# A convolution by Fourier stages beside a gated linear unit: three stages on sums and differences about the middle, and split tokens kept in DRAM

## The chip, the cores and the metric

The kernel runs on one core of a Trainium2 chip. A core has five engines that run their own lists of instructions in order: PE multiplies matrices (its weight loads are the profile's PEld), DVE and ACT work element by element, POOL and SP here mostly issue DMA transfers. The metric is the time of one execution on the device in microseconds (us), the median of several runs.

## The reference

For 2048 tokens of 512 channels the reference computes a gate per token and mixes two branches with it. Branch a is a long convolution of each channel with a kernel built from 128 complex exponentials; branch b is a gated linear unit with 1792 hidden columns.

```python
g = _sigmoid((x * gate_w).sum(-1, keepdims=True))
P = jnp.exp((A * dt[:, None])[:, :, None] * pos[None, None, :])
K = 2.0 * jnp.einsum("dn,dnl->dl", C, P).real
Kf = jnp.fft.rfft(K, 2 * L); Uf = jnp.fft.rfft(u_t, 2 * L)
a = jnp.fft.irfft(Uf * Kf[None, :, :], 2 * L)[:, :, :L] + u * D_skip
b = jnp.einsum("bsf,fd->bsd", (x @ w_gate) * (x @ w_up), w_down)
return g * a + (1 - g) * b
```

## The kernel before, in words

**The gated unit (GLU).** The 1792 hidden columns are 14 tiles f of 128, in five groups (3, 2, 3, 3, 3). Per group, the tokens come as four chunks of 512, so there are 56 steps (one f, one chunk). All three matrices are split into a rounded high part and a low part, and every product is three matmuls (high-low, low-high, high-high). In `hidden` a step has 24 matmuls into the PSUM tiles `pg` and `pu`; their product h is split again by ACT and DVE (`hh`, `hl`), and `down` multiplies it with the split down weights into `y`, 36 matmuls for a chunk and a group of three. A step's results go to DRAM through `acc`; from the second group on by an accumulating DMA of POOL. `tokens` loads 256 KB of one token tile (`raw<-in_xT`), ACT rounds it (`xhi`), DVE subtracts (`xlo`): 16 such tiles in the first group and 12 in each of the other four, since a group begins with the chunk that the one before ended with. Five buffers hold the split token tiles, and a chunk needs four.

**The convolution.** Its 4096-point transform is cut in stages of matmuls between transposes through DRAM. `u_part` reads the tokens and multiplies them with `w1` (8 batches of 4 matmuls, 512 columns each); the result goes to the DRAM tensor `su_d`. For each of 16 blocks of 32 channels DVE and ACT build tables of powers `x` and `v`; `k_block` multiplies them on PE (64 matmuls, "k<-v,x"), and ACT copies the result to `kt` with a transposed order. After every fourth block a quarter q of the channels is ready: `k_first` (two batches with `w1k`) fills `sk_d`; `transforms(q)` runs four batches `m_second` with `w2` on `su_d` and `sk_d`, the complex products `m_product` on DVE, two batches `m_inverse` with `w3` whose results are stored in `y_d`, and `m_last`, which reads `y_d` back (in four loads of 512 KB) and multiplies with `w4`. ACT scales by the gate, and POOL adds the result to the output. All these batches work in the four PSUM banks named `k`, and PE's array is used as several small tiles: for example 64 rows by 32 columns, eight at a time, in `m_second` (`tile_position`).

**Order.** Nothing is left to chance: every piece of work is entered in a list with its engine, a duration, what it reads and writes, and a rank. `Work.run` walks through these with the given durations and writes down the instructions of each engine in the order in which it lets them start. GLU products have the lowest rank and a due time (`T_STEP` times the number of the step, less 5 us). On the chip, each engine then keeps that order and waits by semaphores. The weights of the skip connection (`D_skip`) are loaded once into `skip`, as 4 blocks of 4 short runs. SP issues nearly all loads and stores, one after the other in its own order. A transfer's landing is told by one of eight semaphores, taken in turn, and SP waits for the transfer eight before it on the same semaphore.

Of the kernel before, what the change touches and what calls it, by code (L numbers as in the profile page):

```python
# [10 lines left out]
F32 = mybir.dt.float32  # L11
# [7 lines left out]
P = 128  # L19
# [23 lines left out]
N2 = list(range(1, 32, 2)) + list(range(2, 32, 4)) + list(range(0, 32, 8)) + list(range(4, 32, 8))  # L43
K_COLS = [[(0, 16, 16)], [(32, 8, 40), (48, 4, 52), (56, 4, 60)]]

def fourier_matrices():

    n1, k1 = np.arange(64), np.arange(64)
    ang = 2 * np.pi * np.outer(n1, k1) / 128
    c = np.stack([np.cos(ang), -np.sin(ang)], 2)
    c[:, 0, 1] = (-1.0) ** n1
    c = c.reshape(64, P)
    w1 = np.tile(c, (2, 1))
    w1k = np.tile(np.stack([c[2 * np.array(K_ROWS) + b] for b in range(2)], 1), (4, 1, 1))
    n2, k2 = np.array(N2), np.arange(32)
    w2 = np.zeros((2, 2, 32, 32, 2, 32))  # L60
    w3 = np.zeros((4, 32, 8, 2, 2, 2, 32))
    w4 = np.zeros((P, 64))
    s = 1 / 4096
    for k in range(64):
        S, j, e = k // 8, k // 2 % 4, k % 2
        q = k // 2
        if k:
            ph = 2 * np.pi * np.outer(n2, k + 128 * k2) / 4096
            co, si = np.cos(ph), np.sin(ph)
            w2[e, 0, :, q, 0], w2[e, 1, :, q, 0] = co, si  # L70
            w2[e, 0, :, q, 1], w2[e, 1, :, q, 1] = -si, co
            w3[j, :, S, e, 0, 0], w3[j, :, S, e, 0, 1] = 2 * s * co.T, 2 * s * si.T
            w3[j, :, S, e, 1, 0], w3[j, :, S, e, 1, 1] = -2 * s * si.T, 2 * s * co.T
            w4[2 * k], w4[2 * k + 1] = np.cos(ang[:, k]), -np.sin(ang[:, k])
            continue

        for l in range(1, 32):
            h, f = (0, 128 * l) if l < 16 else (1, 64 + 128 * (l - 16))
            ph = 2 * np.pi * n2 * f / 4096
            co, si = np.cos(ph), np.sin(ph)  # L80
            w2[0, h, :, 0, 0, l], w2[0, h, :, 0, 1, l] = co, -si
            w3[0, l, 0, 0, 0, h], w3[0, l, 0, 0, 1, h] = 2 * s * co, -2 * s * si
        w2[0, 0, :, 0, 0, 0], w2[0, 0, :, 0, 1, 0] = 1.0, (-1.0) ** n2
        w3[0, 0, 0, 0, 0, 0], w3[0, 0, 0, 0, 1, 0] = s, s * (-1.0) ** n2
        w4[0], w4[1] = 1.0, (-1.0) ** n1

    w4 = w4.reshape(2, 4, 2, 2, 4, 64).transpose(0, 2, 1, 3, 4, 5).reshape(P, 64)
    parts = (w1, w1k, w2.reshape(P, 32, 64), w3.reshape(P, 8, 2, 2, 64), w4)
    return [np.ascontiguousarray(a, np.float32) for a in parts]
# [24 lines left out]
T_STEP = 10.3  # L114
# [169 lines left out]
def gated_mix_kernel(  # L284
# [32 lines left out]
    m_su, m_sk, m_y, m_out = (work.memory() for _ in range(4))  # L317
# [12 lines left out]
    def inp(shape):  # L330
        return new("mid", "in", shape, bufs=3)
# [4 lines left out]
    half_pi = const.tile([P, 1], F32, name="half_pi")  # L336
    shift = const.tile([P, 1], F32, name="shift")
    gate = const.tile([P, NR], F32, name="gate")
    ngate = const.tile([P, NR], F32, name="ngate")
    score = const.tile([P, NR], F32, name="score")  # L340
# [4 lines left out]
    w1_t = tpool.tile([P, P], F32, name="w1_t")  # L345
    w1k_t = tpool.tile([P, 2, P], F32, name="w1k_t")
    skip = tpool.tile([P, 4, 32], F32, name="skip")
    m_const, m_powers, m_w1, m_w1k, m_skip = (work.memory() for _ in range(5))
# [3 lines left out]
    gw = new("mid", "bd", [P, D])  # L352
# [22 lines left out]
    def split(hi, lo, s, key):  # L375
# [5 lines left out]
        ph, pl = (hi, s), (lo, s)  # L381
        at = lambda x: x.t if s is None else x.t[:, s * D : (s + 1) * D]
        add("act", 0.62, lambda: act.copy(at(hi), src()), r=[got], w=[ph], rank=0)
        add(
            "dve", 0.69,
            lambda: dve.tensor_tensor(out=at(lo), in0=src(), in1=at(hi).bitcast(F32), op=ALU.subtract),
# [14 lines left out]
    def first_loads():  # L401
        in_y = lambda shape: new("mid", "y", shape, bufs=2)
        in_ev = lambda shape: new("mid", "ev", shape, bufs=3)
# [10 lines left out]
        for f in (1, 2):  # L414
            load_two(lambda k, f=f: ("w", f, k), in_ev, wts[f][:, : 2 * D].rearrange("p (k d) -> p k d", k=2))
# [51 lines left out]
    def product(pg, which, w, x, kt, after, first):  # L467
# [5 lines left out]
        def fn():  # L473
            for n, (a, b) in enumerate(three):
                pe.matmul(
                    pg.t, w[a].t[:, base : base + P], x[b].t, start=kt == 0 and n == 0, stop=kt == KT - 1 and n == 2
                )

        add("pe", 0.681, fn, r=[(w[0], part), (w[1], part), x[0], x[1]], w=[pg], rank=2, after=after)
# [62 lines left out]
    def ends():  # L542
# [7 lines left out]
        for r, y in ending:  # L550
# [4 lines left out]
                    out=sums.t[:, r, P * (KT - 1) :], in0=sums.t[:, r, P * (KT - 1) :], in1=late["fin"].t[:, r],  # L555
# [49 lines left out]

    def u_part(c):
        ut = inp([P, 2, D])
        add("sp", 0.42, lambda: sp.dma_start(ut.t, uv[:, 2 * c : 2 * c + 2, :]), w=[ut], dma=512, after=9.0 + 15.0 * c)

        def score_of(j):  # L610
            r = 2 * c + j
# [4 lines left out]
                    pr.t, ut.t[:, j, :], 1.0, gw.t, op0=ALU.mult, op1=ALU.mult, accum_out=score[:, r : r + 1]  # L616
                ),
                r=[ut, gw], w=[pr, (m_gate, ("s", c // 2))], rank=0,
            )


# [701 lines left out]
```

## Time and profile before

| | |
|---|---|
| median of 3 runs | 618.17 us (617.34 to 620.17) |
| span of the profiled execution | 615.6 us |
| PE busy | 605.5 us (98%) |
| DVE busy | 514.9 us (84%) |
| ACT busy | 420.1 us (68%) |
| DMA | 121.67 MB, 198 GB/s |

The profiled execution has no time of its own beside its span, from the first instruction to the last; the median of the runs is 2.6 us longer. Busy time is the time in which at least one instruction of an engine runs; "idle before" is what the engine waited ahead of a group. All work goes through one recording helper, so the rows carry its line, L100 (L120 after the change), and are told apart by the names of the tiles: out<-in. Names are shown without buffer numbers, so that `w_t` stands for `w1_t` and `w4_t`. An fp32 matmul shows as two records; a GLU matmul (fp32r) as one. A row of the chain of waits gives its start, its length, and the engine and tile that the time went to.

### The profile page before, as it was taken

The numbers are of one execution on the slowest core, as the hardware profiler recorded it, in microseconds if no ns is written. First come the engines' busy times: TensorE is split into PE (matmuls) and PEld (weight loads), VectorE is DVE, ScalarE is ACT, GpSimd is POOL, SyncE is SP. The second block draws the span as 40 slices with busy tenths as digits, with TensorE's granted clock in tenths as the row PEclk, the third lists the DMA queues.
The fourth block names the chain that finished last, engine by engine and source line by source line (L and its number), as shares of the span: only waits on it lengthen the run. The fifth ranks groups of instructions, "written<-read, shape, count | busy, mean of one in ns | idle before, by whom it ended". The sixth has DMA issues, their size and how long they took to land.

```text
span 615.6 us, 17970 instructions
## 1 busy us (share of the span) xinstructions
PE 605.5 (98%) x7524; PEld 468.9 (76%) x7524; DVE 514.9 (84%) x810; ACT 420.1 (68%) x953; POOL 88.6 (14%) x125
## 2 busy tenths in 40 slices
PE   8999999999999999999999999999999999999996
PEld 5776777788777788887768888786888887678865
DVE  6958999999999999999889999999999842377342
ACT  5469877896878886679688768878885663533320
POOL 0211111111112201010120202021110101210120
PEclk9999999999999999999999999999999999999999
DMA  8795736555677977748797939787996789897771
GB/s 284 221 283 181 242 111 199 171 180 119 158 198 189 234 206 191 172 121 206 245 229 181 235 112 229 221 239 167 196 237 194 188 232 308 205 278 199 170 107 69
DMA packets 103238, 121.67 MB, mean 198 GB/s; under 512 B 6644, under 2 KB 66548, under 8 KB 102900
## 3 DMA queue, kind: packets, MB, share of 16 engines
q1 hardware_dynamic: 83732, 92.33, 49.3%
q0 software_dynamic: 19008, 28.06, 25.4%
q8 instruction: 59, 0.97, 0.6%
q14 instruction: 23, 0.19, 0.1%
q10 hardware_dynamic: 416, 0.13, 0.1%
HBM read 69.37 MB, written 51.12 MB: 196 GB/s over the span
## 4 chain that ended last, share of the span: by engine, by line
PE 75%; issue 10%; DMA 7%; DVE 4%; ACT 3%; POOL 1%; POOLq 0%; ACTq 0%; DVEq 0%
PE pg L100 20%; PE y L100 19%; PE pu L100 19%; PE k L100 18%; DMA out<-acc 3%; DMA raw<-in_xT 3%; ACT acc L100 1%; ACT ts L100 1%; DMA y<-in_xT 1%; DVE xlo L100 1%; POOL out L100 1%; ACT rt L100 1%; POOL su_d L100 1%; DVE v L100 1%; DVE t L100 1%
## 5 line engine op out<-in xcount | busy, mean ns | idle before, releaser
L100 POOL DMA_DIRECT2D out<-acc x60 | 51.3, 891 | 369.1 <-ACT acc L100 327.2
L100 PE MATMUL y<-dhi,hl 128*128 128x512 f32 x224 | 90.7, 405 | 1.5 <-ACT acc L100 0.9
L100 PE MATMUL pg<-xhi,wlo 128*128 128x512 f32 x224 | 90.3, 403 | 0.4 <-ACT h L100 0.3
L100 PE MATMUL pg<-xlo,whi 128*128 128x512 f32 x224 | 87.8, 392 | 1.6 <-issue 1.2
L100 PE MATMUL pu<-xhi,wlo 128*128 128x512 f32 x224 | 89.3, 399 | 0.0
L100 PE MATMUL pg<-xhi,whi 128*128 128x512 f32 x224 | 87.7, 392 | 0.5 <-ACT whi L100 0.5
L100 PE MATMUL y<-dhi,hh 128*128 128x512 f32 x224 | 87.5, 390 | 0.0
L100 PE MATMUL y<-dlo,hh 128*128 128x512 f32 x224 | 87.4, 390 | 0.0
L100 PE MATMUL pu<-xhi,whi 128*128 128x512 f32 x224 | 87.4, 390 | 0.0
L100 PE MATMUL pu<-xlo,whi 128*128 128x512 f32 x224 | 87.4, 390 | 0.0
L100 ACT ACTIVATE acc<-y,ngate 128x512 f32<-128x512 f32 x76 | 51.8, 692 | 29.9 <-PE y L100 18.4
L100 DVE TENSOR_TENSOR h<-pu,h 128x512 f32<-128x512 f32 x56 | 38.5, 688 | 39.7 <-PE pu L100 39.4
L100 ACT CAST hh<-h 128x512 fp32r<-128x512 f32 x56 | 34.9, 623 | 38.3 <-DVE h L100 38.2
L100 ACT COPY ts<-k 128x512 f32<-128x512 f32 (+1 forms) x112 | 47.7, 503 | 13.8 <-PE k L100 13.7
L100 PEld LDWEIGHTS y<-dhi,hl 128*128 128x128 f32 x224 | 42.0, 188 | 18.6 <-issue 2.7
L100 PEld LDWEIGHTS pg<-xhi,wlo 128*128 128x128 f32 x224 | 42.1, 188 | 18.1 <-issue 7.8
L100 ACT COPY h<-pg 128x512 f32<-128x512 f32 x56 | 32.9, 588 | 30.7 <-PE pg L100 24.5
L100 PEld LDWEIGHTS pu<-xhi,wlo 128*128 128x128 f32 x224 | 42.0, 188 | 12.7 <-issue 3.0
L100 PEld LDWEIGHTS pg<-xhi,whi 128*128 128x128 f32 x224 | 42.1, 188 | 12.5 <-ACT whi L100 2.1
L100 PEld LDWEIGHTS y<-dhi,hh 128*128 128x128 f32 x224 | 42.0, 188 | 9.3
L100 PEld LDWEIGHTS pu<-xhi,whi 128*128 128x128 f32 x224 | 42.2, 188 | 9.0
L100 PEld LDWEIGHTS pg<-xlo,whi 128*128 128x128 f32 x224 | 42.2, 188 | 8.8 <-DVE xlo L100 0.7
(109 smaller groups left out, 1169.5 us busy)
## 6 DMA issues: line engine op xcount, KB each, us to landing
raw<-in_xT SPq DMA_DIRECT2D x60, 256.0 KB, 4.6
out<-acc POOLq DMA_DIRECT2D x60, 256.0 KB, 6.7
raw<-in_wts SPq DMA_DIRECT2D x36, 256.0 KB, 4.4
su_d<-ts POOLq DMA_DIRECT2D x32, 256.0 KB, 4.6
y_d<-ts SPq DMA_DIRECT2D x16, 512.0 KB, 4.7
sk_d<-ts SPq DMA_DIRECT2D x14, 512.0 KB, 5.3
in<-sk_d SPq DMA_DIRECT2D x12, 512.0 KB, 6.8
in<-su_d SPq DMA_DIRECT2D x12, 512.0 KB, 5.4
```

The costliest lines, as they stand in the source:

```text
L100: got = getattr(self.engine, name)(*args, **kw)
```

## The change

**Sums and differences.** A transform of a sequence about its middle falls into a part of the sums of mirrored points and one of their differences, each with half the matrix.

- `u_part` now takes four token tiles at a time (four loads of 1 MB). DVE forms sums and differences of mirrored tiles (two instructions of 1024 elements and four of 512 per load); two batches of 8 matmuls follow, each 32 rows by 64 columns, 8 tiles of the array at a time. POOL stores the result in 32 transfers as before; these now write runs of 2 KB.
- `k_block`: ACT copies half of the result, DVE writes sum and difference (two instructions of 256 elements per block), with a step of 32 elements between neighbours in `kt`. The table `v` has another order, so that ACT and DVE write some of its parts with steps of 2 and 4 elements.
- `m_second`: 32 matmuls of 256 columns on 16 tiles of 32 by 32, in place of 64 of 128 columns on 8 tiles. `su_d` and `sk_d` are read side by side into one tile.
- `m_last`: 16 matmuls of 512 columns on 8 tiles of 64 by 32, in place of 8 on two tiles of 128 by 64. ACT copies the odd half, DVE forms sum and difference, and the gate is applied in place.
- `k_first`, `m_inverse` and the table products of `k_block` keep their columns.

**Layouts in DRAM.** The lines of `sk_d` and `su_d` are permuted: a store now goes out as 4 blocks of 32 lines. `m_last` reads `y_d` in two loads of 1 MB (for the first three quarters), each as 2 blocks of 64 lines: even lines into the lower 64 partitions, odd lines into the upper.

**Tokens.** High and low part of a token tile share one tile `xs`. In the first group of f it is stored to DRAM after the split (16 stores of 512 KB); from the second group on, 48 loads of 512 KB replace load and split.

**Room and pace.** `in` has 2 buffers instead of 3, `ev` 2, and some small tiles share space; `T_STEP` is 9.85 instead of 10.3.

What stands in SP's row at the end of the first quarter, ahead of `m_last`. Before (`in<-y_d` and `y<-y_d` are the four loads of `m_last`):

```order
L100 DMA raw_3590<-in_xT 128x512
L100 DMA w3s_3597<-in_w3 128x512
L100 DMA w3s_3602<-in_w3 128x512
L100 DMA raw_3609<-in_xT 128x512
L100 DMA y_d_59<-ts_3592 128x8x128
L100 DMA pb_3651<-par_d_90 128x128 x2
L100 DMA y_d_59<-ts_3626 128x8x128
L100 DMA in_3818<-y_d_59 128x2x512
L100 DMA in_3820<-y_d_59 128x2x512
L100 DMA in_3822<-y_d_59 128x2x512
```

The same place of the changed kernel:

```order
L120 DMA y_d_59<-ts_3424 128x8x128
L120 DMA y_d_59<-ts_3443 128x8x128
L120 DMA pb_3584<-par_d_88 128x128 x2
L120 DMA in_3600<-y_d_59 128x1x2048
L120 DMA in_3612<-y_d_59 128x1x2048
L120 DMA xs_3677<-xs_d_60 128x1024
L120 DMA xs_3684<-xs_d_60 128x1024
L120 DMA xs_3701<-xs_d_60 128x1024
L120 DMA xs_3713<-xs_d_60 128x1024
L120 DMA sk_d_58<-ts_3715 4x32x1024
L120 DMA sk_d_58<-ts_3736 4x32x1024
```

Two loads of 1 MB stand where four of 512 KB stood, and behind them now come the loads of the next chunk's split tokens (`xs`) and then the stores of the next quarter's `sk_d`, written as 4 blocks.

On PE, the first product that reads the first of these token tiles, in the changed kernel (`xs_3285` was loaded ahead of the two loads of `y_d`):

```order
L120 MATMUL pg_3740<-xs_3285,wlo_1633 128x512
L120 MATMUL pg_3740<-xs_3285,whi_1623 128x512 x2
L120 MATMUL y_3709<-dhi_2618,hl_3734 128x512
L120 MATMUL y_3709<-dlo_2635,hh_3728 128x512
L120 MATMUL y_3709<-dhi_2618,hh_3728 128x512
L120 MATMUL y_3724<-dhi_2618,hl_3734 128x512
L120 MATMUL y_3724<-dlo_2635,hh_3728 128x512
L120 MATMUL y_3724<-dhi_2618,hh_3728 128x512
L120 MATMUL pg_3740<-xs_3677,wlo_1633 128x512
L120 MATMUL pg_3740<-xs_3677,whi_1623 128x512 x2
L120 MATMUL pg_3740<-xs_3684,wlo_1633 128x512
L120 MATMUL pg_3740<-xs_3684,whi_1623 128x512 x2
```

From the end of the second inverse batch of this quarter to the first product with `xs_3677` there are 102 GLU matmuls and two Fourier batches on PE (before, the split of `raw` by ACT and DVE stood between load and product). `m_last` of quarter 0 on PE, with the rows around it; before:

```order
L100 MATMUL y<-dhi,hl 128x512
L100 MATMUL y<-dlo,hh 128x512
L100 MATMUL y<-dhi,hh 128x512
L100 MATMUL k<-in,w_t 64x512 x6
L100 MATMUL k<-y,w_t 64x512 x2
L100 MATMUL pg<-xhi,wlo 128x512
```

and after:

```order
L120 MATMUL pg<-xs,whi 128x512 x2
L120 MATMUL pu<-xs,wlo 128x512
L120 MATMUL pu<-xs,whi 128x512 x2
L120 MATMUL k<-in,w_t 32x512 x16
L120 MATMUL pu<-xs,wlo 128x512
L120 MATMUL pu<-xs,whi 128x512 x2
```

The eight matmuls became sixteen with 32 instead of 64 rows of output, and the batch now stands inside the products of a step. In the changed kernel it stands 156, 159 and 84 GLU matmuls and four, four and three batches behind the second inverse batch of quarters 0, 1 and 2. In quarters 1 and 2, 18 GLU matmuls after `m_last` begins the next new token tile is read that was loaded behind it in SP's row.

The diff, cut to what is spoken of:

```diff
-T_STEP = 10.3
+T_STEP = 9.85
+U_STEP = 20.0
...
     def inp(shape):
-        return new("mid", "in", shape, bufs=3)
+        return new("mid", "in", shape, bufs=2)
...
     def tokens(gi, ci, kt):
-        x = xs[kt] = [new("glu", n, [P, D], F32R, 5) for n in ("xhi", "xlo")]
+        x = xs[kt] = new("glu", "xs", [P, 2, D], F32R, 5)
+        if gi:
+            add("sp", 0.42, lambda: sp.dma_start(x.t.bitcast(F32), xs_d[ci, kt]), r=[(m_xs, (ci, kt))], w=[x], dma=512, rank=0)
+            return
         load(("x", gi, ci, kt), xT[kt * P : (kt + 1) * P, ci * D : (ci + 1) * D])
-        split(x[0], x[1], None, ("x", gi, ci, kt))
+        split(x, x, (0, 1), ("x", gi, ci, kt))
+        add("sp", 0.42, lambda: sp.dma_start(xs_d[ci, kt], x.t.bitcast(F32)), r=[x], w=[(m_xs, (ci, kt))], dma=512, rank=2)
...
+            add("pe", 1.08, fn, r=[(ut, 2 * s), (ut, 2 * s + 1), w1_t], w=banks, rank=1, hold=[st])
...
-                    lambda h=h, n2=n2, st=st: pool_q.dma_start(
-                        su_d[:, :, n2, :].rearrange("f p d -> p f d"), st.t[:, h].rearrange("p (f d) -> p f d", f=KT)
+                    lambda q=q: pool_q.dma_start(
+                        su_d[q, :, n0 : n0 + 4, :].rearrange("(t a) n d -> a t (n d)", a=4),
+                        st.t[:, q].rearrange("p n d -> p (n d)"),
...
-        add(
-            "act", 1.09,
-            lambda: act.copy(
-                kt.t[:, :, g0 : g0 + 8].rearrange("p n g -> p g n"), pk.t.rearrange("p (g j) -> p g j", j=64)
...
+        add("act", 0.6, lambda: act.copy(side(1), pv(0)[:, :, :, ::-1]), r=[pk], w=[(kt, (1, b % 4))])
+        for h, op in enumerate((ALU.add, ALU.subtract)):
+            add(
+                "dve", 0.45, lambda h=h, op=op: dve.tensor_tensor(out=side(h), in0=pv(1), in1=side(1), op=op),
...
-                        sk_d[q, :, n0 : n0 + 8, :],
-                        st.t.rearrange("p n c g -> p n (c g)"),
+                        sk_d[q, :, n0 : n0 + 8, :].rearrange("(t a) n d -> a t (n d)", a=4),
+                        st.t.rearrange("p n c g -> p (n c g)"),
...
-        add("pe", 2.13, fn, r=[*ins, w], w=banks[0] + banks[1], rank=1, hold=tos, many=apart_of(q))
+        add("pe", 1.15, fn, r=[*parts, w], w=banks, rank=1, hold=[to], many=apart_of(q))
...
-            t = inp([P, 1, 2, 4, P]) if r < 12 else new("mid", "y", [P, 1, 2, 4, P], bufs=2)
-            rows_y = y_d[q].rearrange("k (h r) d -> k h r d", h=2)[:, :, r : r + 4]
+                t = inp([P, 16, P])
+                add(
+                    "sp", 0.42,
+                    lambda t=t, g=g: sp.dma_start(
+                        t.t, y_d[q].rearrange("(k p) n d -> p k (n d)", p=2)[:, :, 16 * P * g : 16 * P * g + 16 * P]
+                    ),
+                    r=[(m_y, (q, T)) for T in range(4)], w=[t], dma=1024,
+                )
```

More of the change, by code (lines that the diff above doesn't have):

```diff
@@ L40, with place, first @@
 K_ROWS = [0, 8, 16, 24] + [i for i in range(32) if i % 8]
-N2 = list(range(1, 32, 2)) + list(range(2, 32, 4)) + list(range(0, 32, 8)) + list(range(4, 32, 8))
-K_COLS = [[(0, 16, 16)], [(32, 8, 40), (48, 4, 52), (56, 4, 60)]]
+def place(tq, t, s1, s2):
+    n1 = 63 * s1 + (1 - 2 * s1) * np.arange(32)
+    pair = 2 * (4 * t + tq)
+    return n1, 31 - pair if s2 else pair
 def fourier_matrices():
[L52 to L60, printed above, removed]
+    k1, th = np.arange(64), 2 * np.pi / 4096
+    def first(a, halves):
+        re, im = np.cos(2 * np.pi * np.outer(a, k1) / 128), -np.sin(2 * np.pi * np.outer(a, k1) / 128)
+        im[:, 0] = np.sin(np.pi * a)
+        order = np.arange(64).reshape(32, 2).T.reshape(64)
+        re, im = re[:, order], im[:, order]
+        return np.concatenate([re, im, -re], axis=1)
+    w1 = np.tile(first(np.arange(32) - 31.5, 2), (4, 1))
+    rows = np.array(K_ROWS)
+    w1k = np.tile(np.stack([first(2 * rows + b - 31.5, 1) for b in range(2)], 1), (4, 1, 1))
+    t = 2 * np.arange(16) - 15.5
+    w2 = np.zeros((2, 2, 2, 16, 32, 32))
@@ L316, in gated_mix_kernel @@
     y_d = dram.tile([KT, P, 32, P], F32, name="y_d")
-    m_su, m_sk, m_y, m_out = (work.memory() for _ in range(4))
+    xs_d = dram.tile([4, KT, P, 2, D], F32, name="xs_d")
+    m_su, m_sk, m_y, m_out, m_xs = (work.memory() for _ in range(5))
     pools = {n: open_pool(n, b, PSUM) for n, b in (("ps_y", 2), ("ps_g", 1), ("ps_k", 4))}
```

470 lines of the change are left out of this document (262 added, 208 removed).

## The prediction

> **What bounds the kernel now.** I read the page's busy times first, then windows of 25 us, then the chain of waits, then the groups by engine and shape, then the transfers. Page and windows (in a window: busy us of PE, PEld, DVE, ACT, POOL, then clock, DMA share, GB/s):
>
> ```profile
> PE 605.5 (98%) x7524; PEld 468.9 (76%) x7524; DVE 514.9 (84%) x810; ACT 420.1 (68%) x953; POOL 88.6 (14%) x125
> 100.00:125.00 25.00, 25.00 (x228) 18.35 (x227) 24.42 (x44) 20.50 (x54) 3.14 (x5) 1.00 0.50 157
> 425.00:450.00 25.00, 25.00 (x466) 20.46 (x465) 23.91 (x37) 22.89 (x66) 6.08 (x6) 1.00 1.00 185
> ```
>
> PE is never free at full clock, and DVE has 0.6 to 1.1 us left of 25. So PE work that is removed counts one to one, as long as DVE and the transfers deliver. The chain gives the prices on PE (start, length, what, records):
>
> ```profile
> 61.45 1.92 PE k L100 x8
> 309.89 3.58 PE k L100 x16
> 356.06 2.00 PE k L100 x124
> 359.64 2.72 PE pg L100 x12
> 398.62 1.93 PE k L100 x16
> ```
>
> Twelve GLU matmuls take 2.72 us, 0.227 each. A batch `u_part` (8 records of 4 matmuls) takes 1.92, `m_last` (16 records of 8) 3.58, `k_first` 1.93, `m_second`, `m_inverse` and the table products 2.00. The first and the last three have 1024 columns on each small tile, `m_last` 2048: about 1.9 us per 1024 columns, whatever the tile's shape.
>
> **PE.** `u_part` goes from 1024 to 512 columns per tile: 8 x 0.96 = 7.7 us less. `m_second` from 1024 to 512: 16 x 1.00 = 16.0. `m_last` from 2048 to 1024: 4 x 1.79 = 7.2. The rest keeps its columns. Sum 30.9. No row has 16 tiles at work; the nearest are those with 8 (`m_second` by 64x32, `m_inverse` by 32x64), which go by their columns, so I take the halved price. The other end is that a 32x32 batch still takes 2.00: 16 us less gain. A gain beyond the columns I exclude, since no shape shows one.
>
> **DVE, ACT and the other transfers.**
>
> ```profile
> L100 DVE TENSOR_TENSOR xlo<-raw,xhi 128x512 fp32r<-128x512 f32 x60 | 40.2, 686 | 10.1 <-ACT xhi L100 9.9
> L100 DVE TENSOR_TENSOR y<-ev 128x1024 f32<-128x1024 f32 x16 | 19.5, 1221 | 3.8 <-ACT ev L100 3.3
> L100 DVE COPY ts<-k 128x256 f32<-128x256 f32 x4 | 1.4, 418 | 3.4 <-PE k L100 3.4
> L100 ACT CAST xhi<-raw 128x512 fp32r<-128x512 f32 x60 | 36.6, 622 | 12.7 <-DMA raw<-in_xT 11.8 <-PE pu L100 0.2
> L100 ACT COPY kt<-k 128x512 f32<-128x512 f32 x16 | 18.0, 1127 | 15.4 <-PE k L100 15.3
> L100 ACT COPY ts<-k 128x512 f32<-128x512 f32 x60 | 31.8, 595 | 8.2 <-PE k L100 8.2
> L100 DVE MEMSET v<- 128x32 f32 x2 | 0.1, 85 | 0.1
> L100 DVE MEMSET half_pi<- 128x1 f32 x1 | 0.1, 59 | 0.0
> ```
>
> DVE loses 48 splits of 0.686 = 32.9 us. It gains in `u_part` 8 x 1.22 + 16 x 0.69 = 20.8, in `k_block` 32 x 0.42 = 13.4, in `m_last` 14 x 0.69 + 4 x 0.42 = 11.3. Net +12.6 on 514.9: 527.5 us, 90% of 585, against 84. It fits, with little to spare: while tables are built it already runs at 96 to 98%, so 0 to 13 us may come through. I take nothing, since PE will wait elsewhere (below). ACT loses 48 x 0.62 and, in `kt`, 16 x some 0.5 us, and gains about 5: some 32 us less, which nobody waits for.
>
> The writes of `k_block` and of `v` with steps could cost more. ACT's transposed `kt` does: 1127 against 595 ns for the same 512 elements, 1.04 ns more for each. Were it so on DVE, 32 x 256 plus 16 x 1536 elements would add 34 us. DVE's own nearest row says no: the memset of 32 elements that lie 64 apart takes 85 ns against 59 for one, 0.84 ns each. I take none. [...]
>
> The tokens add 48 x 256 KB of loads and 16 x 512 KB of stores, 21 MB to 121.7. At the mean share (75% busy) that is hardly free, but the runs are 4 KB long and the loads have a chunk's time; I cost them at nothing, up to 10 us where a load is late. The stores of `su_d` become 4 blocks of 2 KB runs; quarter 0 reads them some 100 us later, so a slower landing costs nothing.
>
> **What is late next: loads in two blocks.** This is the term that decides.
>
> ```profile
> skip<-in_dsk SPq DMA_DIRECT2D x1, 2.0 KB
> ...
> GB/s 0 146 0 0 0 0 0 0 2341 0 0 0 1317 0 0 0 0 0 0 0 0 0 146 0 0 0 0 0 0 0 0 0 0 146 0 2341 0 0 0 0
> DMA packets 7, 0.01 MB, mean 161 GB/s; under 512 B 4, under 2 KB 5, under 8 KB 7
> ...
> q1 hardware_dynamic: 489, 1.69, 74.1%
> ...
> y_d<-ts SPq DMA_DIRECT2D x16, 512.0 KB, 4.7
> in<-y_d SPq DMA_DIRECT2D x9, 512.0 KB, 6.5
> out<-kt SPq DMA_DIRECT2D x4, 256.0 KB, 2.0
> ```
>
> All transfers of before but one have an outermost count of 128, 256 or 32, which 16 engines can share evenly. The one is `skip`: 4 blocks of 4 runs of 128 B. The second and third rows are a window of 0.035 us in its transfer (135.597 to 135.632 us): its four packets under 512 B come one after the other, 9 to 10 ns apart, as on one engine, where 16 engines would have had one packet each. The nearest row for a transfer of 2 blocks is thus one that uses as many engines as it has blocks. From 548.3 to 554.2 us, where the 1 MB of `kt<-out` move in runs of 8 KB, queue q1 moved 1.69 MB at 74.1% of 16 engines: 1.69 / (0.741 x 16 x 5.9) = 24.2 KB per us and engine. So 1 MB on two engines takes 21.7 us, where the four loads of 512 KB landed after 6.5; the pair, on the same two, 43.4; and a store of `sk_d` (4 blocks) 5.4 us on four. The other end: spread over 16 engines, the pair takes 5.4 us and nothing below happens.
>
> [...]
>
> Each engine works off SP's queue in order, so what SP issues behind the pair and spreads over all 16 also waits for the two: the `xs` loads. SP itself stops at the eighth transfer behind the first of the pair, which waits on the same semaphore. From the end of the second inverse batch: eviction 4 x 0.595 = 2.4, store 4.7, pair 43.4, landing 2.0 (the quickest row) = 52.5 us. Against this PE has, in the changed order:
>
> - Quarter 0: 102 GLU matmuls and two batches, 23.1 + 3.9 = 27.0 us, before the first `xs` issued behind the pair is read. Wait 25.5, and 1.4 for the load itself: 26.9.
> - Quarter 1: 159 and four batches before `m_last`, 36.0 + 7.9 = 43.9: wait 8.6. Then 18 GLU matmuls and the batch (6.0) until an `xs` that queues behind three stores of `sk_d` (16.2) and takes 1.4: 11.6. The next `xs` queues behind a fourth store: about 6. Together 26.
> - Quarter 2: 84 and three batches, 19.0 + 5.9 = 24.9: wait 27.6. Then two stores (10.8 + 1.4 - 6.0): 6.2. Together 34.
>
> Quarter 3 reads `y_d` in blocks of 32 lines and is spared. DVE and ACT wait with PE, since the tables have few buffers, so nothing is worked ahead. Sum 87 us.
>
> **Sum.** 615.6 - 30.9 + 87 = 671.7 us of span. The median of the runs stands 2.6 us over the profiled span: 674.
>
> **Rivals.**
>
> - *The loads spread as before* (faster). Then 615.6 - 30.9 + 2.6 = 587, and with DVE's lag and some late `xs` up to 603; say 592. For it speaks that PE's cut is sure; against it, `skip`'s packets. It decides at the pair's time: below 12 us all waits vanish. Chance 0.17.
> - *Only `m_last` waits*, the `xs` loads pass the pair. Then quarter 0 has 156 matmuls and four batches, 43.3 us: 52.5 - 43.3 = 9.2, plus 8.6 and 27.6: 45 us, and 632. No row shows a transfer that overtakes. Chance 0.16.
> - *DVE pays for steps* and the loads are quick: 587 + 34 = 621, no gain left. Chance 0.05, half of it within the bound.
> - The forecast: 0.62.
>
> **Numbers.** Half a percent is about what a measurement of this kernel tells from none. Slower: 0.62 + 0.16 + 0.02 = 0.80; within: 0.03; faster 0.17. For the range of the likeliest case the price per engine counts: by the whole run's row of q1,
>
> ```profile
> q1 hardware_dynamic: 83732, 92.33, 49.3%
> q0 software_dynamic: 19008, 28.06, 25.4%
> ```
>
> it is 92.33 MB / (0.493 x 16 x 615.6 us) = 19.0 KB per us: the pair takes 55 and a store 6.9, 11.8 x 3 + 1.5 x 5 = 43 us more, 717; q0's quarter of the engines on top makes 740. Down it goes to 640 with shorter queues. The second rival, and part of the first rival's upper end, take it to 610.
>
> **What would show it.** In the profile after: `in<-y_d` landing after 20 to 45 us and not 7 (right), or under 8 (then the forecast is wrong); PE `pg` idle on DMA `xs<-xs_d`, and PE `k` idle on DMA `in<-y_d`, 25 to 35 us in each of three places, together 60 to 120; `sk_d<-ts` landing after 6 us or more; PE busy about 30 us less; DVE `kt` at 420 ns (with a penalty for steps 690). I am wrong if two-block loads are spread, or if they end in time because DVE holds PE back anyway.

## The result, and the profile after

The changed kernel takes 776.53 us (median of 4 runs, 774.57 to 783.29), the kernel before, beside it, 617.75 (617.17 to 620.17): 1.257 times the time, with a 95% interval of 1.250 to 1.264. The prediction had the direction and the mechanism; its 674 us gave 56 of the 159 us, and the result lies above the whole of its range, which ended at 740.

The page's busy line of the changed kernel, and what PE waited for (total us, times, longest):

```profile
PE 613.6 (79%) x6500; PEld 456.3 (59%) x6500; DVE 536.6 (69%) x835; ACT 401.0 (52%) x914; POOL 87.3 (11%) x125
...
PE pg L120 <- DMA xs<-xs_d: 44.0, 4, 32.5
PE k L120 <- DMA in<-y_d: 33.4, 2, 20.4
PE k L120 <- ACT ts L120: 24.0, 1, 24.0
PE k L120 <- DMA in<-sk_d: 14.6, 2, 10.1
PE k L120 <- issue: 9.7, 3, 9.3
PE pu L120 <- DVE h L120: 6.0, 3, 4.9
PE y L120 <- DVE kt L120: 5.5, 1, 5.5
```

PE is idle for 772.9 - 613.6 = 159.3 us, against 10.1 before. The first two rows are the waits that the prediction named. They come in the same three places: 32.5 us at 329 us (split tokens behind the first pair of `y_d` loads), 24.0 at 494 (the third row) and 7.0 at 532, 13.0 and 20.4 at 633 and 648 (the third quarter's `m_last`), with 4.0 and 0.6 for split tokens just behind. The rows below the third were in no term of the sum. The wait at 494 us took another form than predicted: PE waits for ACT, which waits for a stage tile `ts` that a store of `sk_d` still reads.

SP's own row after the first quarter (start, length, transfers):

```profile
319.90 22.66 SPq L120 DMA_DIRECT2D xs<-xs_d  x4
342.66 32.11 SPq L120 DMA_DIRECT2D sk_d<-ts  x4
377.02 1.64 SPq L120 DMA_DIRECT2D raw<-in_wts  x2
```

SP takes 22.7 us to issue four loads and 32.1 us for four stores: it is itself held up, so everything behind it is late, not the two transfers alone.

Windows of the changed kernel (PE, PEld, DVE, ACT, POOL busy, then granted clock, DMA share, GB/s):

```profile
325.00:350.00 25.00, 4.08 (x19) 3.04 (x17) 16.27 (x25) 8.68 (x19) 1.75 (x2) 0.67 0.53 142
500.00:525.00 25.00, 7.16 (x147) 6.19 (x148) 6.14 (x8) 6.23 (x15) 0.29 (x1) 0.58 0.38 129
650.00:675.00 25.00, 6.89 (x34) 4.14 (x34) 1.76 (x3) 2.19 (x6) 0.86 (x1) 0.57 0.43 139
...
361.60:366.60 5.00, 5.00 (x12) 3.64 (x12) 0.00 (x0) 0.00 (x0) 0.00 (x0) 0.50 0.14 56
```

The last row begins where the wait of 32.5 us ends. PE is busy throughout, at a granted clock of 0.50, and does 12 matmuls in 5 us where twelve took 2.72.

Two more windows show how many DMA engines work around that wait. In the first the pair of `y_d` loads moves alone; in the second the stores of `sk_d` move beside it:

```profile
316.00:330.00 14.00, 12.89 (x64) 9.23 (x62) 13.96 (x18) 9.25 (x21) 0.00 (x0) 1.00 0.13 52
348.00:358.00 10.00, 0.00 (x0) 0.00 (x0) 0.00 (x0) 0.00 (x0) 0.00 (x0) 0.50 0.25 100
```

The DMA share is 0.13 and then 0.25, as much as 2 and 4 of 16 engines give that work without pause. The packets of 8 KB, which only these loads have in SP's queue here, begin at 314.2 us and end at 359.8: 45.6 us for the pair. PE's wait for the first split tokens that SP issued behind the pair ends at 361.6 us, 1.8 us after the last of these packets.

DVE and the transfers of `su_d` did what the prediction had excluded or taken as free:

```profile
L120 DVE TENSOR_TENSOR kt<-k,kt 128x256 f32<-128x256 f32 x32 | 21.6, 674 | 3.6 <-ACT kt L120 3.4
L120 DVE TENSOR_TENSOR v<-v,sq 128x512 f32<-128x512 f32 x16 | 11.0, 690 | 0.0
L120 DVE TENSOR_TENSOR v<-v,sq 128x256 f32<-128x256 f32 x16 | 10.2, 638 | 1.5 <-ACT sq L120 1.5
...
su_d<-ev POOLq DMA_DIRECT2D x32, 256.0 KB, 14.1
```

Operations that write with a step of 32 elements (`kt`) cost 674 ns and not 420; with a step of 4 (`v`, 256 elements) 638 against 421 before; with a step of 2 (`v`, 512 elements) 690 against 685. The stores of `su_d` land after 14.1 us; before it was 4.6.

### The profile page after: what moved, and what is told of

The parts are those of the page before. It is cut to its first block, busy times and chain, and to the rows that moved or that the text cites. A ratio compares the mean times of both kernels' runs of the same rounds, so it can differ in the third digit from the quotient of the medians.

```text
span 772.9 us, 15856 instructions
## 1 busy us (share of the span) xinstructions
PE 613.6 (79%) x6500; PEld 456.3 (59%) x6500; DVE 536.6 (69%) x835; ACT 401.0 (52%) x914; POOL 87.3 (11%) x125
## 5 line engine op out<-in xcount | busy, mean ns | idle before, releaser
L120 PE MATMUL pg<-xs,whi 128*128 128x512 f32 x448 | 142.8, 400 | 2.2 <-issue 1.3
L120 PE MATMUL pu<-xs,whi 128*128 128x512 f32 x448 | 140.8, 396 | 0.0
L120 PE MATMUL pg<-xs,wlo 128*128 128x512 f32 x224 | 92.4, 413 | 44.6 <-DMA xs<-xs_d 44.0
L120 PEld LDWEIGHTS pg<-xs,whi 128*128 128x128 f32 x448 | 86.8, 194 | 22.1 <-ACT whi L120 1.8
L120 PE MATMUL pu<-xs,wlo 128*128 128x512 f32 x224 | 91.9, 410 | 6.0 <-DVE h L120 6.0
L120 PEld LDWEIGHTS pu<-xs,whi 128*128 128x128 f32 x448 | 86.1, 192 | 17.4
L120 PEld LDWEIGHTS pg<-xs,wlo 128*128 128x128 f32 x224 | 43.1, 193 | 64.2 <-DMA xs<-xs_d 46.6
L120 ACT COPY ev<-k 128x512 f32<-128x512 f32 x88 | 47.0, 595 | 26.1 <-PE k L120 26.1
L120 PEld LDWEIGHTS pu<-xs,wlo 128*128 128x128 f32 x224 | 42.9, 192 | 26.0 <-issue 8.4
L120 PEld LDWEIGHTS k<-v,x 128*32 128x32 f32 x2048 | 33.5, 116 | 32.1 <-ACT ts L120 24.8
L120 PEld LDWEIGHTS y<-dlo,hh 128*128 128x128 f32 x224 | 43.5, 194 | 10.1 <-DVE dlo L120 2.2
## 6 DMA issues: line engine op xcount, KB each, us to landing
su_d<-ev POOLq DMA_DIRECT2D x32, 256.0 KB, 14.1
```

The costliest lines, as they stand in the source:

```text
L120: got = getattr(self.engine, name)(*args, **kw)
```

## Experiments: which transfers cost the 159 us

The first theory (A) is the prediction's: transfers of 2 and 4 blocks use few DMA engines, and all that SP issues behind them waits. Its rival (B): the time comes from the new orders and layouts, however the transfers are cut. The first three kernels change only how a transfer is cut.

**Each 1 MB load of `y_d` as two loads of 64 lines.**

```diff
-lambda t=t, g=g: sp.dma_start(t.t, y_d[q].rearrange("(k p) n d -> p k (n d)", p=2)[:, :, 16*P*g : 16*P*g + 16*P])
+lambda t=t, g=g: [sp.dma_start(t.t[64*p : 64*p + 64],
+    y_d[q].rearrange("(k p) n d -> p k (n d)", p=2)[p, :, 16*P*g : 16*P*g + 16*P]) for p in range(2)]
```

> The changed kernel, with each 1 MB load of y_d for the last stage cut into two loads of 64 lines (one for the even lines, one for the odd); all engines keep their order. Theory A (a transfer of two blocks runs on two DMA engines, and what SP issues behind it waits for those two): the waits of PE on xs behind y_d (33 and 7 us) and of the last stage on y_d (33 us) go, with what follows from them (the 24 us of the table product that waits for the stage buffers of sk_d partly stays): 70 to 100 us less, 675 to 705 us. Theory B (the added 21 MB of transfers and the fewer buffers are the cause): within 15 us of 776.

Measured: two runs, 691.55 and 701.94 us, 85 and 75 us less than the changed kernel. Both lie in the range of theory A and far from that of B.

**Each store of `sk_d` as four stores of 32 lines.**

```diff
-sp.dma_start(sk_d[q, :, n0 : n0 + 8, :].rearrange("(t a) n d -> a t (n d)", a=4), st ...)
+[sp.dma_start(sk_d[q, :, n0 : n0 + 8, :].rearrange("(t a) n d -> a t (n d)", a=4)[a], st[32*a : 32*a + 32] ...) for a in range(4)]
```

> The changed kernel, with each store of sk_d cut into four stores of 32 lines of 4 KB; the loads of y_d stay in two blocks. Theory A: the stores leave four engines for all sixteen, so the waits on sk_d (10 and 5 us of the second stage, part of the 24 us of the table product) go, while the waits behind y_d stay: 20 to 50 us less, 725 to 755 us. Theory B: within 15 us of 776.

Measured: 738.65 us, ratio to before 1.194 (1.188 to 1.199), 38 us less than the changed kernel, as theory A says. In its list of transfers the cut stores land after 4.9 us:

```profile
sk_d<-ts SPq DMA_DIRECT2D x56, 128.0 KB, 4.9
```

**Both cuts, and the stores of `su_d` cut in four as well.**

> Both cuts, and the stores of su_d cut into four of 32 lines as well; same order on PE, DVE and ACT. Theory A: nothing waits on y_d, sk_d or xs behind them for more than some us, PE's clock stays full, and the kernel ends where PE and DVE bound it: 590 to 610 us, faster than before by 1 to 4.5%. Theory B: above 700 us.

Measured: 635.01 us, 1.027 (1.022 to 1.032). The three cuts give 142 of the 159 us back, and a pair of `y_d` loads now moves in 10 to 11 us. But A had expected the kernel to come out ahead of the one before, and it is 17 us behind. That rest is the subject of the next section.

**The loads of `y_d` issued by POOL, still in two blocks.**

```diff
-lambda t=t, g=g: sp.dma_start(t.t, y_d[q] ...)
+lambda t=t, g=g: pool_q.dma_start(t.t, y_d[q] ...)
```

> The changed kernel, with the two loads of y_d issued by POOL in place of SP, still in two blocks. If the xs loads wait because they stand behind y_d in the same queues of SP, their waits (33 and 7 us) go although y_d itself takes as long, and the last stage still waits some 30 us: 720 to 750 us. If it is the two engines' work as such, whatever queue it comes from, xs still waits (the engines take queues in turn, so perhaps half as long): 750 to 790 us.

Measured: 728.61 us, 1.177 (1.170 to 1.185). Out of SP's queue the same loads hold up 48 us less, so what stands behind them in SP's queue is a part of the damage. How large a part is not shown, since from POOL's queue the pair itself moved in 28 to 34 us and not in 45. That the DMA engines take queues in turn shows in the changed kernel: from 339.5 to 340.7 us, while the pair moves, packets of 2 KB of POOL's queue (6) and of 8 KB of SP's (5) begin by turns, two and two, and the two `out<-acc` that POOL issued at 330 us land after 8.7 and 12.5 us, ahead of the pair. In e4 the trace also has the landing of the `y_d` loads:

```profile
in<-y_d POOLq DMA_DIRECT2D x6, 1024.0 KB, 35.2
```

35.2 us is the median of the six. It is not the landing that the prediction priced, which was from SP's queue.

## Experiments: why spread transfers do not bring the gain

With everything spread, PE has some 22 us less to do than before (below), and the kernel is still slower. The windows of the kernel before, and then of the spread one, show where:

```profile
25.00:100.00 75.00, 74.29 (x436) 54.63 (x435) 64.76 (x115) 56.89 (x136) 17.19 (x24) 1.00 0.67 214
100.00:500.00 400.00, 397.47 (x5656) 314.50 (x5655) 378.75 (x565) 310.36 (x716) 53.28 (x60) 1.00 0.76 193
600.00:616.00 16.00, 10.92 (x47) 8.37 (x45) 4.32 (x6) 0.99 (x2) 0.00 (x0) 0.97 0.18 67
```

```profile
25.00:100.00 75.00, 66.39 (x324) 46.74 (x323) 65.15 (x120) 49.56 (x121) 39.54 (x80) 0.91 0.85 277
100.00:500.00 400.00, 398.56 (x4892) 307.33 (x4891) 393.77 (x579) 300.17 (x694) 71.73 (x100) 1.00 0.85 215
600.00:625.00 25.00, 9.05 (x100) 3.78 (x101) 10.25 (x20) 2.31 (x5) 2.90 (x2) 0.58 0.49 115
```

Between 100 and 500 us PE is full in both, and DVE now is too (98%). The losses are at the start, where 227 GLU matmuls are done between 25 and 100 us instead of 266, and at the end, where PE waits 9.3 us for the last `m_last` and 5.5 us behind it and runs at a clock of 0.58. Counted in the trace, the list has 1728 of 2016 GLU matmuls ahead of the last table product (at 516 us), where the kernel before had 1659 (at 503 us). Behind that product the last quarter's chain takes 114 us, with 288 GLU matmuls (65 us) to cover it. So the PE time that was saved had been filled with GLU work, which was then missing at the end. Theories for why: DVE's tables are late (C), or start, transfers and order set the pace (S).

**`kt` in runs of 8.** The same values at the same places, with the elements in another order.

```diff
...
-side = lambda h: kt.t[:, h, :, :, g0 : g0 + 8].rearrange("p b k g -> p g b k")
+side = lambda h: kt.t[:, h, :, :, g0 : g0 + 8].rearrange("p b k g -> p (b k) g")
...
```

> Base: the kernel with all transfers spread (635.0 us). One edit: ACT and DVE write `kt` in runs of 8 neighbouring elements instead of with a step of 32, the same values at the same places. Theory C (between 100 and 510 us DVE is the bound, busy 24 to 25 of 25 us, so the last table product, now at 514 us against 501 before, and all behind it move with DVE): if the price of a step belongs to each write that leaves the line of the one before, DVE's `kt<-k,kt` falls from 675 ns to 420 to 500, 32 x 0.2 = 6 us, the last table product comes at 508 and the time is 626 to 631. Rival S (the start and the transfers set the pace, DVE only follows): the row falls, the time stays within 2 us of 635. If the row stays at 675, the order of the elements is not what costs, and nothing follows for C.

Measured: 634.34 us, 1.026 (1.022 to 1.029); the last table product stays at 515 us. The row falls all the way:

```profile
L120 DVE TENSOR_TENSOR kt<-k,kt 128x256 f32<-128x256 f32 x32 | 13.3, 417 | 3.0 <-ACT kt L120 3.0
```

8.3 us less on DVE are worth nothing, which speaks against C. This edit is in all kernels from e8 on but e15.

**The tokens' part alone**, in the kernel before: split once, 16 stores, 48 loads.

> The kernel before with the tokens' part of the change alone: split once, stored in 16 transfers, loaded split from the second group on; DVE 33 us and ACT 30 us less, 21 MB more to move. If the transfers cost nothing, as the prediction has it, PE is the bound as before and the time is 614 to 621. If the 8.4 MB of stores in the first 100 us hold up the start (there the kernel with all transfers spread has done 227 GLU matmuls between 25 and 100 us, against 266 before), it is 624 to 632.

Measured: 639.04 us, 1.032 (1.029 to 1.035): 21 us slower, with 29 us less on DVE, and above both ranges that I gave. At 100 us it is 30 GLU matmuls (6.8 us) behind; over the whole span PE is idle 14 us more and busy 8 us longer, and no wait is over 4 us. The tokens' part was not free here.

**The Fourier part alone** (e3 with tokens loaded and split in each group).

> The kernel with all transfers spread (635.0 us), without the tokens' part: tokens are loaded and split in each group as in the kernel before, so DVE has 33 us more and the transfers 21 MB less. Theory C (DVE is the bound between 100 and 510 us): the last table product comes 20 to 33 us later than at 514 us, and the time is 650 to 668, with PE's busy time still some 24 us under that of before in matmuls. Rival S (start and transfers set the pace): 618 to 632, since the stores of the first 100 us are gone.

Measured: 653.68 us, 1.056 (1.052 to 1.060), the last table product at 562 us, later than C had it. This does not show that DVE holds the tables back: the list, made anew, puts 1908 GLU matmuls ahead of that product, 180 more than in e3, and these alone are 41 of the 46 us. The product comes where the list puts it: 1443 and 447 us in e6, 1728 and 516 in e3. Either part alone costs more (21 and 36 us) than both together (17).

**A candidate** with the loads of `y_d` cut, `w1k`'s columns in the order of the lines of `sk_d` (so that its stores need no cut; `ps` shares the buffer of `sq` to make room), `su_d` uncut, and prices nearer the measured ones for `m_second` and the squares of `v` in the list.

> The changed kernel with y_d's loads in two halves, `w1k`'s columns in the order of the lines of sk_d (so that a store has 128 lines one after the other and needs no cut), su_d's stores as in the changed kernel, `kt` in runs of 8, and the list's durations set to what was measured for m_second (1.5) and the squares of `v` (0.65 to 0.71). If transfers, DVE and the start's POOL work explain what was left over: 610 to 626. If the price of the last quarter's chain stays (waits of 9.3 and 5.5 us, clock 0.58): 626 to 640.

Measured: 640.50 us, 1.036 (1.032 to 1.040), half a microsecond above the second range. With these prices the list puts still more GLU work ahead (1743), the last table product comes at 525 us, and with `su_d` in few blocks waits of 4.6 and 3.0 us return at 62 to 68 us.

**Spread without more transfers.** As the candidate, with the list's old prices, and `su_d` goes out in four stores by blocks of lines instead of by quarters.

```diff
-            for q in range(KT):
+            for a in range(4):
...
-                        su_d[q, :, n0 : n0 + 4, :].rearrange("(t a) n d -> a t (n d)", a=4),
-                        st.t[:, q].rearrange("p n d -> p (n d)"),
+                        su_d[:, a::4, n0 : n0 + 4, :].rearrange("q t n d -> t q (n d)"),
+                        st.t[32 * a : 32 * a + 32].rearrange("p q n d -> p q (n d)"),
```

> The changed kernel with every transfer spread but no more transfers than it has (y_d's loads in two halves; `w1k`'s columns in the order of sk_d's lines; su_d stored in four transfers by blocks of lines instead of four by quarters) and `kt` in runs of 8. Against the kernel with all transfers spread by cutting (634 us): POOL's busy time falls from 128 to about 88 us, and if it was POOL's slower work on four times the transfers that kept `ev` full and PE waiting 5 us at 81 us, that gap is gone and the time is 624 to 630. If not, 632 to 638.

Measured: 631.68 us, 1.021 (1.016 to 1.026). The wait of 5 us at 81 us is gone, and 265 GLU matmuls are done between 25 and 100 us. The time is 2 us above the range I gave: the end is as it was, with waits of 9.2 and 5.5 us.

**The first stores of tokens later, and another loop order in `m_second`.**

> e9 with two edits in separate places. The stores of the split tokens are entered no earlier than 26 us, so that the four of the first chunk (2 MB) no longer stand at 9 us ahead of the loads of weights and parameters. If these stores are what held up the start, PE does 20 to 30 GLU matmuls more between 25 and 50 us than the 64 to 67 of now, and the time is 4 to 7 us under e9; if it is the loads' own mass, no change. And m_second issues its 32 matmuls with the column group as the innermost loop instead of the row group: if the order of issue sets its price, the batch falls from 1.42 towards 1.00 us (the last quarter gains 2 us at most); if the 16 tiles themselves share something, it stays at 1.42.

Measured: 642.73 us, 1.040 (1.035 to 1.044). Neither outcome that I gave for the stores came: the time rises by 11 us against e9. The list made anew has a wait of 7.2 us for ACT's `xs` at 42 us, and 47 GLU matmuls between 25 and 50 us instead of 67. `m_second` keeps its price whichever index runs innermost, the second of the two outcomes: 385 ns a record in both orders.

**Four GLU steps less** (the 14th tile of f is left out).

```diff
-GROUPS = [range(0, 3), range(3, 5), range(5, 8), range(8, 11), range(11, 14)]
+GROUPS = [range(0, 3), range(3, 5), range(5, 8), range(8, 11), range(11, 13)]
```

> e9 without the last of the 14 tiles of f (the last group has two), so that four steps and 144 GLU matmuls, 32.7 us of PE, are left out, all of them behind 450 us. Theory T (the end is set by the chain from the last table product through the last quarter, not by PE's amount of work): the time falls by less than 10 us against e9. If PE's work sets the end, it falls by 25 to 33 us.

Measured: 617.45 us, 1.000 (0.997 to 1.002): 14 of 32.7 us, between the two. The last table product stays at 514 us and the chain behind it, up to PE's last product, shrinks from 112 to 100 us. So the chain sets most of the end, and the GLU work that stands inside it on PE seems to lengthen it; the two are not told apart further.

**Two of DVE's sums on POOL.**

> e9 with late stores of the first split tokens and the sums `su` and `di` (0.76 and 0.52 us per block on DVE, 20 us in all) formed by POOL. If DVE's own time sets when the last table product comes, DVE's busy time falls by 20 us, that product comes at 495 to 505 instead of some 513 us, and the time is 610 to 622. If POOL is slow or DVE's instructions get slower beside it, the last product stays and the time is that of e10, 622 to 632, or above.

Measured: 651.51 us, 1.054 (1.049 to 1.059), 9 us above e10, whose late stores it shares. POOL takes 1.70 us for what took DVE 0.76, and DVE's small products take 829 ns on average instead of 361 in e10. Of the 30 of them, 14 overlap POOL's sums and take 1368 ns on average; the other 16 take 358. DVE's busy time rises to 543.3 us:

```profile
L124 POOL TENSOR_TENSOR su<-ri 128x576 f32<-128x576 f32 x16 | 27.1, 1695 | 90.5 <-DVE ri L124 90.5
...
L124 DVE TENSOR_TENSOR sq<-pb,ri 128x192 f32<-128x192 f32 x30 | 23.8, 829 | 0.2
```

**Raw tokens at the end.** The last two chunks of the last group load 256 KB a tile and split it, as before.

```diff
+        if gi == 4 and ci >= 2:
+            load(("x", gi, ci, kt), xT[kt * P : (kt + 1) * P, ci * D : (ci + 1) * D])
+            split(x, x, (0, 1), ("x", gi, ci, kt))
+            return
```

> e9 (631.7 us), but the last two chunks of the last group load their tokens as before (256 KB each) and split them on ACT and DVE, which have time there: eight loads of 512 KB become eight of 256 KB, 2 MB less beside the last quarter's transfers; DVE has 5.5 us more. If the loads of split tokens hold up the last quarter, the stores of sk_d land there after 7 to 10 us instead of 13 to 15, m_second of that quarter starts 5 to 10 us earlier than at 559, and the time is 620 to 628. If only DVE's tables set the end, it stays at 630 to 634.

Measured: 622.93 us, 1.008 (1.005 to 1.011), 8.8 us less than e9 and inside the range, though not by the row I named. SP's row around the last stores of `sk_d` in e9, and then here:

```profile
521.86 4.47 SPq L124 DMA_DIRECT2D xs<-xs_d  x3
528.42 0.32 SPq L124 DMA_DIRECT2D sk_d<-ri  x1
530.77 0.32 SPq L124 DMA_DIRECT2D sk_d<-e  x1
546.04 1.00 SPq L124 DMA_DIRECT2D x<-sk_d  x2
```

```profile
525.85 0.33 SPq L124 DMA_DIRECT2D sk_d<-ri  x1
526.51 0.33 SPq L124 DMA_DIRECT2D sk_d<-e  x1
536.36 1.78 SPq L124 DMA_DIRECT2D raw<-in_xT  x2
540.79 1.00 SPq L124 DMA_DIRECT2D x<-sk_d  x2
```

The stores still land after 13.3 to 14.2 us, where 7 to 10 was expected. But they are issued 3 to 4 us earlier, with no loads of split tokens ahead of them, and what reads them follows 5 us earlier.

**Less work on DVE**: `su` and `di` formed for the first block only, in e9 and in the kernel before.

```diff
     def direct_powers(b):
...
+        if b:
+            sus[b] = sus[0]
+            return
     su, di = sus[b] = new("tab", "su", [P, TB, 18]), new("tab", "di", [P, TB, 11])
```

> e9, but the sums `su` and `di` are formed for the first block alone and used for all (so the tables of the other blocks are other numbers): 15 x 1.28 = 19 us less on DVE, all of it ahead of the last table product. If DVE's time per block is what holds that product back, it comes 8 to 19 us earlier than at 511 and the time is 612 to 624. If not (PE's order, the transfers), 628 to 634.

> The kernel before with the same sums left out: 19 us less on DVE. PE is busy 98% of the span there, so the last table product may come earlier, but the time stays: 613 to 619. If it fell by 8 us or more, DVE and not PE would have been the bound of the kernel before as well, and the premise of the prediction, that PE work counts one to one, would have been wrong from the start.

Measured: e14 629.12 us, 1.019 (1.016 to 1.022): DVE's busy time falls by 15 us (529.8 to 514.4), which brings the last table product from 513 to 509 us and 2.6 us of time, so C falls as the cause of what is left. The list has 1707 GLU matmuls ahead of that product, 24 fewer than in e9, which is 5.4 us of PE. e15 616.85 us, 0.999 (0.996 to 1.001), as expected: with 15 us less on DVE the kernel before stays as it is, so it was not DVE that bound it.

**The list's numbers.** e13 with other durations (e16), and e13 with another pace (e17: `T_STEP` 10.5 instead of 9.85).

```diff
-add("pe", 0.681, fn, ...)          # product and down
+add("pe", 0.7, fn, ...)
-add("pe", 1.15, fn, r=[*parts, w], ...)   # m_second
+add("pe", 1.45, fn, r=[*parts, w], ...)
```

> e13 (622.9 us) with two numbers of the list changed: three GLU matmuls are entered at 0.70 us (measured with what stands between them) instead of 0.681, and m_second at 1.45 instead of 1.15. The order then has 1680 GLU matmuls ahead of the last table product instead of 1731, and the products of the last quarter have more GLU work around them. If the order is what leaves PE dry at the end, the last table product comes at or before 511 us, the wait ahead of the last m_last falls from 4.2 us, and the time is 612 to 620. If the last quarter's chain sets the end whatever stands around it, 620 to 628.

> e13 (622.9 us) with the pace T_STEP at 10.5 instead of 9.85 (the kernel before had 10.3): 1704 GLU matmuls ahead of the last table product instead of 1731. The pace is part of the change; if it was it that pulled GLU work ahead, the time is 612 to 620; if the tables on DVE do it anyway, 620 to 628.

Measured: e16 617.65 us, 1.000 (0.998 to 1.003); e17 622.06 us, 1.009 (1.007 to 1.011). Numbers that tell the list what PE's work takes bring the last table product to 500 us, with 1680 matmuls ahead, and the wait ahead of the last `m_last` is gone; the pace alone does nothing. What is left of waits in e16:

```profile
PE y L124 <- DVE kt L124: 5.5, 1, 5.5
PE y L124 <- ACT acc L124: 3.0, 3, 1.7
```

**The last two additions swapped**, in e16: DVE first empties PSUM, then adds the last quarter's rows.

> e16 with one edit at the very end: of the two additions that make the last four tiles of the output, DVE now first takes `y` out of PSUM (times ngate, plus the sums read back) and then adds the rows of the last m_last, instead of the other way round, so that PE's last products no longer wait for the last quarter. If that wait is the whole of what is left, PE's last product moves ahead of or beside the last m_last, the gap of 5.5 us and the slow products behind it go, and the time is 605 to 612, 1 to 2% under before. If the last quarter's chain (m_last at 593 to 603 us) sets the end anyway, the sums and the stores behind it still stand there and the time is 613 to 617.

Measured: 615.29 us, 0.995 (0.993 to 0.998), the only version whose interval lies ahead of the kernel before, by half a percent. The wait of 5.5 us is gone, PE is done at 602 us and not 609, and DVE's last addition ends at 606.2 us instead of 610.1. Only some 2 us of that reach the time: behind PE's last product still come the last quarter's rows and their stores. The time lies at the upper outcome of the two that I gave.

## Why the prediction was wrong in size

**The direction and the mechanism were right.** Loads in two blocks and stores in four, and what queues behind them, cost 142 of the 159 us (e3). The pairs of `y_d` loads took 45.6, 45.4 and 45.0 us in the three quarters, with a DMA share of 0.13 (2 in 16) where they moved alone, against 43.4 us in the prediction. That both loads of a pair move on the same two engines, which the 43.4 us rest on, no row of the kernel before shows; it was an estimate of mine, and the share of 0.13 bears it out. PE waited in the three places named, by quarter 32.5, 31.0 and 38.0 us, where 26.9, 26 and 34 were forecast. In quarter 1 that nearness is partly luck: `m_last` did not wait there at all, and 24.0 of the 31.0 us are a wait for `ts` that the prediction did not have.

**The step that failed is the sum of the waits, "Sum 87 us".** PE's idle time rose by 149 us, 62 more than that. In the three places the waits are 101.5 us, 14.5 more than 87. Another 29.4 us had no term: 14.6 for loads of `sk_d`, read soon after they were stored (10.1 of it before the first pair of `y_d` loads); 9.3 and 5.5 in the last quarter, which the prediction called spared and where e3 waits as long with every transfer spread. The last 159.3 - 101.5 - 29.4 = 28.4 us are smaller waits, 18 more than before had in all. The sentence that DVE and ACT wait with PE, "so nothing is worked ahead", was given no price; a wait can then also move the tables, and with them the next quarter, but no run shows that by itself.

**The term for PE was too large, and the cost of a wait behind it was missing.** PE's busy time did not fall by 30.9 us but rose by 8.1; this is the other 39 us of the 101 by which the span was missed. Rows per batch, before and then in e18, where no long wait disturbs them:

```profile
L100 PE MATMUL k<-in,w2s 64*32 64x128 f32 x1536 | 25.0, 272 | 0.0
L100 PE MATMUL k<-in,w_t 64*128 64x512 f32 x64 | 15.9, 615 | 0.0
```

```profile
L124 PE MATMUL k<-in,w2s 32*32 32x256 f32 x768 | 17.9, 385 | 0.0
L124 PE MATMUL k<-in,w2s 32*64 32x512 f32 x128 | 10.1, 613 | 0.7 <-DVE in L124 0.7
L124 PE MATMUL k<-in,w_t 64*32 64x512 f32 x96 | 5.8, 595 | 0.0
```

`m_second` went from 25.0 / 12 = 2.08 to 17.9 / 12 = 1.49 us, 0.59 less and not 1.00; `u_part` from 15.9 / 8 to 10.1 / 8, 0.73 less and not 0.96; `m_last` to 5.8 / 3 = 1.93, against 3.58 in the chain before, 1.65 less, near the 1.79 (the row counts the tail of the last product, the chain does not). Together 16 x 0.59 + 8 x 0.73 + 4 x 1.65 = 22 us and not 30.9: the truth for `m_second` lies between the halved price that was taken and the other end that was kept (no gain). Even so PE's busy time is 613.6 us, where 605.5 - 22 would be 583: some 30 us are matmuls that take longer behind the waits, as in the row with the clock at 0.50. In the whole trace PE is busy for 54 us at that clock, about half of which (27 us, an estimate from the clock of 0.50) is time lost. Behind the wait of 24.0 us the clock is back at 1.00 after 3.4 us of work, behind the wait of 32.5 us, where matmuls keep a spacing of 0.43 us, after 6.0, and a wait of 4.0 us at 675 us already costs 6.0 us at half clock.

**DVE's steps: I took the wrong row.** A memset of 32 elements stood for a two-input operation of 256. The price is there, 8.2 us in `kt` and 6.8 in `v`, and ACT's row, which I set aside, was the right neighbour. It comes to 15 us and not to the 34 of the calculation that I rejected, since the operations of 512 elements with a step of 2 pay nothing. DVE's busy time is 536.6 us, where 527.5 was forecast. In these rows a step of 8 bytes costs nothing (690 against 685 ns for 512 elements), steps of 16 and of 128 bytes cost 0.85 and 1.0 ns an element (638 against 421 ns and 674 against 417, for 256), and runs of 32 bytes nothing (417 ns in e5). What `kt`'s steps cost the kernel is little: without them the time is the same (e5: 634.34 us, e3: 635.01).

**The tokens were not free.** "At nothing, up to 10" was 21 us alone in the kernel before (e6), and e13, which loads the last eight token tiles unsplit, is 8.8 us faster than e9. Beside the Fourier part they still gain: without the tokens' part e3 takes 19 us longer (e7).

**The faster rival was priced wrong.** Spread loads were to give 592 us and gave 632 to 635. It rested on "PE work that is removed counts one to one". PE is busy 98% of the span before, and e15 shows that DVE was no bound there, but the sentence needs something that keeps PE busy to the end. After the change the list spent the saved time on GLU work ahead of the tables, and the chain of the last quarter ended uncovered.

What stays open: how e6's 21 us divide beyond the 7 at the start; why the list still puts 1707 GLU matmuls ahead of the last table product when DVE has less to do (e14); and whether a shorter chain behind the last table product would turn e18's lower PE time (586.8 us busy against 605.5) into time.

## What to carry to other kernels

For each transfer look at the outermost count on both sides, and then at all that stands behind it in its queue: the loads of 1 MB in 2 blocks, 45 us a pair, cost more (75 to 85 us by e1) than the 22 us of PE time that the change saved. An engine's time that is saved is gained only if the chain that ends last gets shorter; count what is left to cover that chain before and after. When operations get cheaper, give the planner their measured prices first: e13 and e16 differ by two durations and 5 us.

## What the runs showed of the hardware

- A batch of `m_second` on 16 tiles of 32 by 32 takes 1.49 us for 512 columns a tile, where 8 tiles took 2.08 for 1024; in both orders of issue a record takes 385 ns (e9, e10).
- DVE reads PSUM with a step of 64 elements at no extra cost: in e5 it reads `k` so, and takes 417 ns, where the copy of 256 neighbours from `k` took 418 before.
- Work on POOL slows some of DVE's instructions beside it: in e12 products of 192 elements take 1368 ns where they overlap POOL's sums (of 1695 and 1239 ns), and 358 where they do not.
- Behind each wait of 4 us or more in the changed kernel (4.0 to 32.5 us) PE's granted clock is still 0.50 for 3 to 7 us, or until the next wait.
- Two loads of two blocks, 2 MB in all, took 45 us at a DMA share of 0.13 (2 in 16); cut into loads of 64 lines they took 10 to 11 us (e3; in e9 four such loads landed after 8.9 us, their median).
